# A convolution and an expert layer in one kernel: parts of 28 rows of tokens in place of 14, and more blocks of four units

## The chip, the cores and the metric

The kernel runs on one core of a Trainium2 chip. The time is that of one execution on the device, in microseconds (us); 1278.25 is the median of three runs before the change (1277.03 to 1278.94). A core has five engines that run side by side, each through its own list of instructions in order: PE (matmuls), DVE (vector), ACT (activation), POOL (here: scatters and a few sums) and SP (issues most DMAs). An instruction waits at the head of its engine until the semaphores that it names are reached, and everything behind it waits too.

## What is computed

```python
w = softmax(weight, -1)                       # 8 heads x 7 taps
x = sum over k of w[h, k] * x_pad[b, s + k]   # causal, (8, 3584, 192)
logits = x @ w_gate                           # 8 experts
local_gate = sigmoid(x @ w_local)
for b, s:                                     # e is kept along a sequence
    e = argmax(logits[b, s]) if s == 0 or local_gate[b, s] < 0.5 else prev_e
    out[b, s] = softmax(logits[b, s])[e] * (relu(x[b, s] @ w1[e]) @ w2[e])
    prev_e = e
```

The heads have 24 channels each, w1 is 192 x 1024 and w2 is 1024 x 192 for each expert, all in fp32. Tokens number 28672. A token takes the expert of the token before it unless its own gate opens, so routing is a scan along each sequence of 3584.

## The kernel before

**Parts.** Tokens are worked through in 16 parts of 1792, two to a sequence. Parts 0 and 1 are convolved on PE at the start (`wide`, `wide_route`). The others are convolved by `conv` on DVE: a partition holds 14 tokens in a row with a halo of 6, laid out as six chunks of 32 channels; for each chunk ACT makes the first tap and DVE adds six, each an operation of 128x448 (L441). `route` then takes the logits on PE (`logits`, L632), turns the convolved rows to token order on DVE (L642), scans the experts and works out for each token a slot in a table in DRAM, sorted by expert. `put` scatters one row of 128 tokens into `slots`, on POOL (L846): 14 of them a part.

**Blocks.** The expert layer runs over units of 128 tokens of one expert, in blocks: singles (one unit) first, then pairs, then quads (four units, `seven` and `output_late`), and at the end late pairs and late singles for what is left in each expert. `table` finds after each part which full units there are and which expert each block takes. `ONE`, `TWO` and `MID` say how many blocks of a kind have to be there after part g; `_sure` counts those that exist whatever the routing, `_likely` those that exist if the routing is not far out. A block that was only likely may stay empty; as many spare blocks (`LOSE`, `SPARE`) stand behind an `if` at the end. Each block loads the w1 and w2 of its expert, 1.5 MB.

**Order.** All instructions are recorded in one hand-made order, the order of each engine's list. The loop over blocks calls `hidden` and `output` (or `seven` and `output_late`), and in between `step(time)`: it takes convolution or routing operations from two generators (`conv`, `route`) until their planned times (0.68 for an L441 operation, 0.2 for a small one) fill the given time. So `step`'s numbers say how much of DVE's side work stands in each block. `start_route` waits until the rows tile is free (`rows_free`), `start_conv` until the part before has been turned. `spots` in `output` name the matmuls behind which a `put` follows. `ensure(i)` loads the rows of the blocks after i (`load_rows`); when those of the next one or two blocks still lack scatters, it records the missing `put`s on the spot. `load_rows` waits for all scatters of its part.

**Buffers.** x of a part has two tiles; the rows in token order have three (`row_tile`), z (the convolved part) two, and the quads' rows take over one of them.

Of the kernel before, what the change touches and what calls it, by code (L numbers as in the profile page):

```python
# [8 lines left out]
F32 = mybir.dt.float32  # L9
I32 = mybir.dt.int32  # L10
# [14 lines left out]
NT = 14  # L25
PT = P * NT
NPART = N // PT
PER = S // PT
# [18 lines left out]
EARLY = 2  # L47
SINGLES = 21
# [9 lines left out]
def _likely(tokens, size, left):  # L58
# [7 lines left out]
NARROW = 8  # L66
PAIRED = 46
# [20 lines left out]
LOSE = 4 * LOST + 2 * LOST2  # L88
# [7 lines left out]
TQ = (NT + 3) // 4  # L96
WA = F * KD // 2
# [14 lines left out]
def kernel(  # L112
# [118 lines left out]
    def z_tile():  # L231
        return yt.tile([P, 3 * NH * TB + NB * DR], F32, name="z")
# [181 lines left out]
    def conv(g, x_sb):  # L414
        z = (z_tile() if g % 2 else
             ys[2].tile([P, NB, DG], F32, name="y_sb").rearrange("p b d -> p (b d)"))
        z = z[:, :NT * D].rearrange("p (b s) -> p b s", b=DQ)
# [16 lines left out]
        for b in range(DQ):  # L434
            at["b"] = b
            firsts(0 if 0 < st["block"] < TURNED else 1)
            if b == {3: 3, 4: 3}.get(g, 1) and 2 < g < NPART - 1:
                x_in[g + 1] = load_x(g + 1)
                st["loaded"] = st["block"]
            for k in range(1, KC):  # L440
                nc.vector.scalar_tensor_tensor(z[:, b, :], chans(b, k), c[:, b, k:k + 1],  # L441
                                               z[:, b, :], Alu.mult, Alu.add)
                yield 0.68
# [168 lines left out]

    def gathered(ps):
        xg = xp.tile([P, KT, DG], F32, name="xg")
# [4 lines left out]
    def logits(g, z):  # L619
# [27 lines left out]
        nc.vector.transpose(lq.rearrange("p t e -> p (t e)"), ls.rearrange("p h x -> p (h x)"))
        yield 0.4
        lt = sm.tile([P, NT, E + 1], F32, name="lt")
        aside = g > ASIDE and (st["cgen"] is not None or not late_p)  # L650
        if aside and late_p:
            yield "hop"
        for r in range(4):
# [11 lines left out]
            if aside:  # L665
                yield "hop"
        return y_sb, lt

    def route(g):
        y_sb, lt = yield from logits(g, got.pop(g))  # L670
# [3 lines left out]
        yield 0.3  # L674
        ex = sm.tile([P, NT, E], F32, name="ex")
        nc.vector.tensor_tensor(ex, lg, bcast(mx, E), op=Alu.subtract)
        yield 0.3

        eq = sm.tile([P, NT, E], F32, name="eq")
        nc.vector.scalar_tensor_tensor(eq, ex, 0.0, bcast_mid(ed, NT), Alu.is_equal, Alu.mult)  # L680
        yield 0.3
        key = sm.tile([P, NT], F32, name="key")
        nc.vector.tensor_reduce(key, eq, axis=AX.X, op=Alu.max)
        yield 0.3
# [3 lines left out]
        if g % PER == 0:  # L688
# [971 lines left out]
```

## Time and profile before

| | |
|---|---|
| median of three runs | 1278.25 us |
| the profiled execution | 1279.44 us, its span 1277.7 us |
| granted PE clock | 0.996 |
| DVE convolution operations (L441) | 504 of 0.70 us |
| DMAs of weights | 105 of 1536 KB, 12 of 512 KB |
| scatters into slots | 228 |

The page's first part gives each engine's busy time and share of the span; its second cuts the span into 40 slices (a digit is tenths of busy time). The view by stages lists for each stretch its length, then for each engine the busy time with its number of records, the granted PE clock, the share of the DMA engines and GB/s. In the timeline and in the chain a row has its start, its length, engine, line, what is written `<-` what is read, the number of instructions merged, and in brackets the idle time before it with what ended it. A matmul in fp32 leaves two records. In a group's row the two numbers behind the first bar are busy us in all and the mean of one in ns.

### The profile page before, as it was taken

What the parts mean: (1) busy time and instruction counts of PE and PEld (TensorE: products, weight loads), DVE (VectorE), ACT (ScalarE), POOL (GpSimd) and SP (SyncE); (2) the same over time, 40 slices, a digit from 0 to 9 for tenths busy, and PEclk for the clock granted to TensorE, in tenths of its full rate; (3) what the DMA queues carried; (4) which work ended last, traced back from release to release, by engine and by line L of the source; (5) the groups of instructions that cost most, each with busy time, mean ns of one, the idle gap of its engine ahead of it and who ended that gap; (6) DMA issues with size and microseconds to landing.
All of it is one profiled execution on the core that took longest, in us unless ns stands there. A gap on an engine that the chain in (4) does not pass through costs nothing.

```text
span 1277.7 us, 39046 instructions
## 1 busy us (share of the span) xinstructions
PE 1251.7 (98%) x15186; PEld 1204.5 (94%) x15186; DVE 957.8 (75%) x2507; ACT 535.5 (42%) x1164; POOL 556.9 (44%) x619
## 2 busy tenths in 40 slices
PE   8899999999999999999999999999999999999997
PEld 7889998999999999999999999999999999999996
DVE  6989887999998989999899989985886443431111
ACT  5445542333343442434434544544444453432332
POOL 4544452434344444444446355536456533321211
PEclk9999999999999999999999999999999999999998
DMA  5799988979798898979897564636466464456894
GB/s 202 266 368 417 360 292 284 343 231 308 222 296 263 256 288 239 292 251 270 284 243 232 120 176 125 179 103 195 131 163 178 137 168 126 124 154 199 259 302 155
DMA packets 185810, 293.96 MB, mean 230 GB/s; under 512 B 150416, under 2 KB 160839, under 8 KB 170386
## 3 DMA queue, kind: packets, MB, share of 16 engines
q1 hardware_dynamic: 163296, 246.18, 61.5%
q0 software_dynamic: 22320, 45.22, 10.8%
q8 instruction: 121, 1.98, 0.6%
q14 instruction: 71, 0.58, 0.1%
q10 hardware_dynamic: 2, 0.00, 0.0%
HBM read 245.75 MB, written 46.07 MB: 228 GB/s over the span
## 4 chain that ended last, share of the span: by engine, by line
PE 83%; DVE 9%; DMA 4%; issue 2%; POOL 0%; SPq 0%; ACT 0%; DVEq 0%; POOLq 0%
PE ps L1299 22%; PE yps L1102 19%; PE hps L1078 18%; PE ps L1249 14%; PE ps L1194 4%; PE xps L1249 3%; DVE y_sb L441 2%; DMA wb<-in_w_dram 2%; DVE z L441 1%; DMA hot<-slots 1%; DMA y_sb<-slots 1%; PE xps L632 1%; DVE o_sb L1116 1%; PE hps L252 1%; DMA slots<-y_sb,posi 1%
## 5 line engine op out<-in xcount | busy, mean ns | idle before, releaser
L1130 POOL DMA_INDIRECT out_dram<-o_sb,head x208 | 215.3, 1035 | 455.7 <-DVE o_sb L1314 265.8
L1102 PE MATMUL yps<-wb,hT 64*128 64x192 f32 x3616 | 317.6, 324 | 5.3 <-DVE o_sb L1116 4.8
L1078 PE MATMUL hps<-xT,wb 64*128 64x256 f32 (+1 forms) x3216 | 312.5, 344 | 1.3 <-issue 1.1
L1102 PEld LDWEIGHTS yps<-wb,hT 64*128 64x128 f32 x3616 | 302.0, 187 | 12.1 <-DVE o_sb L1116 9.9
L1299 PE MATMUL ps<-wb,hot 64*128 64x192 f32 x3712 | 310.6, 323 | 0.0
L846 POOL DMA_INDIRECT slots<-y_sb,posi x228 | 232.4, 1019 | 167.6 <-PE yps L1102 70.8
L1299 PEld LDWEIGHTS ps<-wb,hot 64*128 64x128 f32 x3712 | 302.3, 187 | 3.0 <-issue 0.6
L1078 PEld LDWEIGHTS hps<-xT,wb 64*128 64x128 f32 x3216 | 280.9, 187 | 21.3 <-issue 1.6
L1087 ACT ACTIVATE hT<-hps 128x512 f32<-128x512 f32 (+1 forms) x268 | 127.4, 527 | 164.0 <-PE hps L1078 163.9
L441 DVE SCALAR_TENSOR_TENSOR z<-x_sb,c,z 128x448 f32<-128x448 f32 x252 | 175.1, 704 | 12.2 <-ACT z L428 6.1
L441 DVE SCALAR_TENSOR_TENSOR y_sb<-x_sb,c,y_sb 128x448 f32<-128x448 f32 x252 | 174.0, 700 | 10.8 <-ACT y_sb L428 4.9
L1314 DVE SCALAR_TENSOR_TENSOR o_sb<-ps,head,o_sb 128x192 f32<-128x192 f32 x116 | 43.5, 412 | 125.2 <-ACT o_sb L1309 119.9
L1309 ACT ACTIVATE o_sb<-ps,head 128x192 f32<-128x192 f32 x116 | 43.2, 417 | 204.9 <-PE ps L1299 204.9
L1112 ACT ACTIVATE o_sb<-yps,head 128x192 f32<-128x192 f32 x92 | 33.6, 417 | 163.0 <-PE yps L1102 162.9
L1173 DVE STREAM_TRANSPOSE xT<-y_sb 128x768 f32<-128x768 f32 (+1 forms) x65 | 55.2, 877 | 62.1 <-PE ps L1194 28.6
L1249 PE MATMUL ps<-xT,wb 64*128 64x256 f32 x736 | 88.6, 377 | 0.0
L1249 PEld LDWEIGHTS ps<-xT,wb 64*128 64x128 f32 x736 | 77.5, 187 | 1.2 <-issue 0.4
L1194 PE MATMUL ps<-xT,wb 64*128 64x128 f32 (+1 forms) x912 | 67.3, 300 | 0.9 <-DVE xT L1173 0.9
L1194 PEld LDWEIGHTS ps<-xT,wb 64*128 64x128 f32 x912 | 65.2, 188 | 1.8 <-DVE xT L1173 1.8
L1270 DVE TENSOR_TENSOR hot<-xps,hot 128x512 f32<-128x512 f32 x46 | 31.5, 685 | 42.0 <-PE xps L1249 42.0
L1271 ACT ACTIVATE hot<-hot 128x512 f32<-128x512 f32 x46 | 29.0, 630 | 64.3 <-DVE hot L1270 64.3
L1059 DVE STREAM_TRANSPOSE xT<-hot 128x768 f32<-128x768 f32 x46 | 44.6, 971 | 9.7 <-DMA hot<-slots 9.6
(301 smaller groups left out, 1363.5 us busy)
## 6 DMA issues: line engine op xcount, KB each, us to landing
wb<-in_w_dram SPq DMA_DIRECT2D x105, 1536.0 KB
x_sb<-in_x_dram SPq DMA_DIRECT2D x14, 1920.0 KB
hot<-slots SPq DMA_DIRECT2D x184, 96.0 KB
y_sb<-slots SPq DMA_DIRECT2D x92, 192.0 KB
wb<-in_w_dram SPq DMA_DIRECT2D x12, 512.0 KB
slots<-y_sb,posi POOLq DMA_INDIRECT x228
out_dram<-o_sb,head POOLq DMA_INDIRECT x208
x_sb<-in_xb_dram SPq DMA_DIRECT2D x4, 768.0 KB
```

Source lines behind the costliest of these rows:

```text
L441: nc.vector.scalar_tensor_tensor(z[:, b, :], chans(b, k), c[:, b, k:k + 1], z[:, b, :], Alu.mult, Alu.add)
L846: ins = nc.gpsimd.indirect_dma_start(out=slots[:, :], in_=rows, in_offset=None, out_offset=bass.IndirectOffsetOnAxis(ap=to, axis=0)).ins
L1059: nc.vector.transpose(xT.rearrange("p d (j t) -> p j d t", t=Q), xgs[i][0].rearrange("p j (d t) -> p j d t", t=Q))
L1078: ins = nc.tensor.matmul(hps[half][:, j, w], lhsT=wb[rows, w1 + f0:w1 + f0 + P], rhs=xT[rows, d, w], start=(d == 0 and j == 0), stop=(d == ...
L1087: nc.scalar.activation(hT[:, m:m + 2, w], hps[half][:, :, w], Act.Relu)
L1102: ins = nc.tensor.matmul(yps[half][:, k * D:(k + 1) * D], lhsT=hT[rows, m, k * P:(k + 1) * P], rhs=wb[rows, w2 + m * D:w2 + (m + 1) * D], ...
L1130: sent = nc.gpsimd.indirect_dma_start(out=out, in_=o, in_offset=None, out_offset=bass.IndirectOffsetOnAxis(ap=xg.bitcast(I32)[:, k, 1:2], ...
L1173: nc.vector.transpose(xT.rearrange("p d (j t) -> p j d t", t=Q)[:, js], rows[:, js].rearrange("p j (d t) -> p j d t", t=Q))
L1194: nc.tensor.matmul(hps[:, half, j, :], lhsT=wb[rows, f0:f0 + P], rhs=xT[rows, d, :], start=(d == 0 and j == 0), stop=(d == KD - 1), skip_g ...
L1249: ins = nc.tensor.matmul(to[:, half, j, :], lhsT=b[rows, j * P:(j + 1) * P], rhs=a[rows, :], start=(first and j == 0), stop=True, skip_gro ...
L1299: ins = nc.tensor.matmul(yps[:, half, k * D:(k + 1) * D], lhsT=h[two][rows, side, j, k * P:(k + 1) * P], rhs=wb[rows, f * D:(f + 1) * D], ...
L1314: nc.vector.scalar_tensor_tensor(o_sb[:, k, :], yps[:, 1, k * D:(k + 1) * D], xg[:, at + k, 0:1], o_sb[:, k, :], Alu.mult, Alu.add)
```

## The change

Parts 2 to 15 become seven parts of a whole sequence: 28 tokens in a row on each partition (`NT`), still six chunks, with operations of 128x896 (L472 in the new file). Seven tiles' worth of buffers become one tile, `arena`, in which places are given by hand: six chunk places for x, each loaded again for the next part as soon as its convolution is over (`load_chunk`, one DMA a chunk); one z; three halves of a part's rows as a ring (`row_tiles`, `H_AT`), of which a part takes two; a place for the quads' rows and one for temporaries. `so_far` is no longer carried from part to part, as a part is a sequence.

The blocks are 23 singles, 20 pairs, 28 + 8 quads, 4 late pairs and 42 late singles of which 28 are spare; before they were 21, 46, 19 + 4, 5 and 34 of which 20 are spare. Two of the singles and three of the first 12 pairs are now likely and no longer sure. 7, 14 and 23 singles come from the two halves of sequence 0 as before, 12 pairs from sequence 1, 8 from sequence 2, then 7 quads from each of the next four.

The times of `step` change: 2.2 + 2.8 planned us in a single (before 2.1 + 1.2 + 1.3), 3.9 + 1.2 + 3.3 in a pair (before 4.2 + 1.2 + 3.4), 10.7 in a quad as before; a 128x896 operation counts as 1.15. `spots` get more places for scatters, as 28 of them follow each route.

```diff
-NT = 14
-PT = P * NT
-NPART = N // PT
+PT = P * 14
+NT = 28
+EARLY = S // PT
+NPART = EARLY + (N - S) // (P * NT)
...
-PAIRED = 46
+PAIRED = 20
...
+    def load_chunk(g, b):
+        if g < NPART:
+            nc.sync.dma_start(out=spot(X_AT + b * XN, XN),
+                              in_=x[g - EARLY, :, b * XN:(b + 1) * XN])
...
-        return ys[(0, 1, 3)[g % 3] if g < NARROW else g % 2].tile([P, NB, DG], F32, name="y_sb")
+        return spot(g * YN, YN).rearrange("p (b d) -> p b d", d=DG)
+
+    def row_tiles(g):
+
+        return [spot(H_AT[(2 * (g - EARLY) + k + 2) % 3], HN).rearrange("p (b d) -> p b d", d=DG)
+                for k in range(2)]
...
-        return not any(p[0] <= (g - 3 if g < NARROW else g - 2) for p in to_put)
+        return (not any(p[0] <= g - 2 for p in to_put)
+                and (g == EARLY or sum(p[0] == g - 1 for p in to_put) <= HT))
...
-            if b == {3: 3, 4: 3}.get(g, 1) and 2 < g < NPART - 1:
-                x_in[g + 1] = load_x(g + 1)
-                st["loaded"] = st["block"]
+            load_chunk(*((g, b + 4) if b < 2 else (g + 1, b - 2)))
             for k in range(1, KC):
                 nc.vector.scalar_tensor_tensor(z[:, b, :], chans(b, k), c[:, b, k:k + 1],
                                                z[:, b, :], Alu.mult, Alu.add)
-                yield 0.68
+                yield 1.15
...
-        if to_put and to_put[0][0] == 3:
+        if n == 1 and len(to_put) > 3 * (TURNED - 1 - st["block"]):
+            spots[2, 0, 7] = 0
+        if to_put and (to_put[0][0] == EARLY or n > 1 and len(to_put) > HT):
...
-            if j >= FIRST and j > i + 2:
+            if j >= FIRST and j > i + 2 or j > FIRST > i:
                 return
...
-            step((2.4, 0)[i] if i < 2 else 2.1 if n == 1 else 4.2 if i < FIRST - 1 else 3.0)
+            step((2.4, 0)[i] if i < 2 else 2.2 if n == 1 else 3.9 if i < FIRST - 1 else 3.0)
...
-                step(1.3 if n == 1 and i != 1 else 3.4)
+                step(3.4 if i == 1 else 2.8 if n == 1 else 3.3)
```

How the instructions stand, at two places. First POOL, at the end of the singles. `slots<-` are scatters of rows (`put`), `out_dram<-o_sb,xg` the outputs of singles, `out_dram<-o_sb,head` those of pairs; the brackets hold what an instruction waits for. Before, from the output of the last single to the first of the first pair:

```order
L1130 DMA out_dram<-o_sb,xg 28672x192 [waits DMAHW2_49,DMASW0_49,DVE_49]
L846 DMA slots<-y_sb,posi 230528x195 [waits DMASW1_49,PE_49]
L846 DMA slots<-y_sb,posi 230528x195 [waits DMASW2_49,PE_49]
L846 DMA slots<-y_sb,posi 230528x195 [waits DMASW3_49,PE_49]
L846 DMA slots<-y_sb,posi 230528x195 [waits DMASW4_49,PE_49]
L846 DMA slots<-y_sb,posi 230528x195 [waits DMASW5_49,PE_49]
L1130 DMA out_dram<-o_sb,head 28672x192 [waits DMAHW1_49,DMASW6_49,DVE_49]
```

With the change, the last rows of the singles and the first of the pairs:

```order
L876 DMA slots<-arena,posi 230528x195 [waits DMASW5_49,PE_49]
L876 DMA slots<-arena,posi 230528x195 [waits DMASW6_49,PE_49]
L876 DMA slots<-arena,posi 230528x195 [waits DMASW7_49,PE_49]
L1157 DMA out_dram<-o_sb,xg 28672x192 [waits DMAHW7_49,DMASW0_49,DVE_49]
L876 DMA slots<-arena,posi 230528x195 [waits DMASW1_49]
L1157 DMA out_dram<-o_sb,xg 28672x192 [waits DMAHW1_49,DMASW2_49,DVE_49]
L1157 DMA out_dram<-o_sb,head 28672x192 [waits DMAHW3_49,DMASW3_49,DVE_49]
```

Before, the scatters between the last single and the first pair belong to part 3, while the first pair takes rows of part 2, scattered blocks earlier. Now the one scatter between the outputs of singles 21 and 22 is the last of part 2 (all of sequence 1), recorded by `ensure` and so with no matmul to stand behind; the first pair's rows are loaded behind it.

Second DVE, in a quad beside convolution. `hot<-` are the sums of the first layer, `xT<-` the transposes of the next block's rows, `xg`, `xT` and `hT` from `xT` the next block's combined rows, `o_sb` the outputs. Before, from one block's transposes on:

```order
L1173 STREAM_TRANSPOSE xT<-y_sb 128x8x3x32 x2
L441 SCALAR_TENSOR_TENSOR y_sb<-x_sb,c,y_sb 128x448 x10
L1314 SCALAR_TENSOR_TENSOR o_sb<-ps,head,o_sb 128x192 x2
L1224 TENSOR_TENSOR xg<-xT 128x256
L1225 TENSOR_TENSOR xT<-xT 128x256
L1226 TENSOR_TENSOR xg<-xT 128x256
L1228 TENSOR_TENSOR hT<-xT,xg 128x256
L1229 TENSOR_TENSOR hT<-xT 128x256
L441 SCALAR_TENSOR_TENSOR y_sb<-x_sb,c,y_sb 128x448 x3
L1314 SCALAR_TENSOR_TENSOR o_sb<-ps,head,o_sb 128x192 x2
L441 SCALAR_TENSOR_TENSOR y_sb<-x_sb,c,y_sb 128x448 x3
L1270 TENSOR_TENSOR hot<-xps,hot 128x512
```

With the change:

```order
L1198 STREAM_TRANSPOSE xT<-arena 128x8x3x32 x2
L472 SCALAR_TENSOR_TENSOR arena<-arena,c 128x896 x6
L1339 SCALAR_TENSOR_TENSOR o_sb<-ps,head,o_sb 128x192 x2
L1249 TENSOR_TENSOR xg<-xT 128x256
L1250 TENSOR_TENSOR xT<-xT 128x256
L1251 TENSOR_TENSOR xg<-xT 128x256
L1253 TENSOR_TENSOR hT<-xT,xg 128x256
L1254 TENSOR_TENSOR hT<-xT 128x256
L472 SCALAR_TENSOR_TENSOR arena<-arena,c 128x896
L1339 SCALAR_TENSOR_TENSOR o_sb<-ps,head,o_sb 128x192 x2
L472 SCALAR_TENSOR_TENSOR arena<-arena,c 128x896 x2
L1295 TENSOR_TENSOR hot<-xps,hot 128x512
```

Where 16 operations of 448 stood between two blocks' transposes, 9 of 896 stand now, at the same three places.

More of the change, by code (lines that the diff above doesn't have):

```diff
@@ L24 @@
 UT = 128
-NT = 14
-PT = P * NT
-NPART = N // PT
-PER = S // PT
+PT = P * 14
+NT = 28
+HT = NT // 2
+EARLY = S // PT
+NPART = EARLY + (N - S) // (P * NT)
+TOK = [PT * (g + 1) if g < EARLY else S + P * NT * (g + 1 - EARLY) for g in range(NPART)]
 HALO = KC - 1
@@ L46 @@
 DUMMY = E * CAPU
-EARLY = 2
-SINGLES = 21
 SPARE = 2
@@ L96 @@
 TQ = (NT + 3) // 4
+YN = NB * DG
+HN = HT * DG
+RN = QT // Q * D2
+R_AT = 2 * HN
+H_AT = (0, HN, R_AT + RN)
+XN = NX * Q
+X_AT = H_AT[2] + HN
+Z_AT = X_AT + DQ * XN
+ZN = NT * Q
+TMP_AT = Z_AT + DQ * ZN
+ZW = 3 * NH * TB + NB * DR
+TMP = (("ls", 2 * TQ * Q), ("lq", 2 * TQ * Q), ("lt", NT * (E + 1)), ("ex", NT * E), ("eq", NT * E),
+       ("oh", NT * E), ("at", NT * E))
+ARENA = TMP_AT + sum(n for _, n in TMP)
 WA = F * KD // 2
@@ L664, in logits @@
                     yield 0.12
-            if aside:
+            if aside and r % 2:
                 yield "hop"
-        return y_sb, lt
+        return y_sbs, lt
     def route(g):
-        y_sb, lt = yield from logits(g, got.pop(g))
+        y_sbs, lt = yield from logits(g, got.pop(g))
         lg = lt[:, :, :E]
@@ L813, in route @@
         for t in range(NT):
-            to_put.append((g, y_sb[:, t, :], posi[:, t:t + 1]))
+            to_put.append((g, y_sbs[t // HT][:, t % HT, :], posi[:, t:t + 1]))
         yield 0.2
@@ L1061, in turn_pair @@
         return xT
-    def few():
-        return to_put and to_put[0][0] == 2 and st["block"] % 2 == 0
     def hidden(n, wb, xT, w1):
@@ L1082, in hidden @@
                     held.pop(0)(ins)
-                if n == 1 and (two, d) == (0, 0) and st["block"] and not (st["hot"] or few()):
+                if n == 1 and (two, d) == (0, 0) and st["block"] and not st["hot"]:
                     put(ins)
@@ L1147, in ring @@
             return flat[:, at:at + n * UT // Q * D2].rearrange("p (j d) -> p j d", d=D2)
[L1148 to L1151 removed]
+        flat = room["rows"] if (i - FIRST) % 2 else spot(R_AT, RN)
+        return flat[:, :n * UT // Q * D2].rearrange("p (j d) -> p j d", d=D2)
     def make_room():
@@ L1157, in make_room @@
             room[f"h{k}"] = flat[:, k * 4 * HU * P:(k + 1) * 4 * HU * P]
-        small = [xp.tile([P, KT, DG], F32, name="xg").rearrange("p k d -> p (k d)")[:, :HU * P]
-                 for _ in range(5)]
+        small = [xp.tile([P, HU * P], F32, name="xg") for _ in range(5)]
         room["wt"], room["xc"] = small[:3], small[3:]
@@ L1164, in more_room @@
         room["xc"] += [flat[:, k * HU * P:(k + 1) * HU * P] for k in range(2)]
+        room["rows"] = flat[:, 2 * HU * P:]
     def turn_late(n, rows):
@@ L1324 @@
     late_p = []
-    LATE = 3
     SIDE = (2.4, 4.5, 2.0, 1.8)
     st = {"block": 0, "conv": 1, "cgen": None, "route": 1, "rgen": None, "routed": 1,
-          "due": False, "hot": False, "since": 0, "bank": None, "over": 0, "turned": 1, "loaded": 0}
+          "due": False, "hot": False, "since": 0, "bank": None, "over": 0, "turned": 1}
     def start_conv():
         g = st["conv"] + 1
-        if (st["cgen"] is None and g < NPART and g <= st["turned"] + 2
-                and (late_p or g < 4 or st["block"] > st["loaded"] + 2)
-                and (g != 3 or g in x_in and st["block"] > LATE + 2)):
+        if st["cgen"] is None and g < NPART and g <= st["turned"] + 1:
             st["conv"] = g
-            st["cgen"] = conv(g, x_in.pop(g))
+            st["cgen"] = conv(g)
             next(st["cgen"])
@@ L1376, in step @@
             elif c == "pe":
-                st["due"], st["since"], go = True, st["block"] - early, False
+                st["due"], go = True, False
+                st["since"] = st["block"] - (early or time > 1.5)
             elif c == "hop":
@@ L1383, in step @@
                 time -= c + 0.05 if go and late_p else c
-        st["over"] = min(time, 1.5) if late_p else 0
+        st["over"] = min(time, 1.5) if late_p else min(time, 0)
     ya, yb = row_tile(0), row_tile(1)
@@ L1541, in between @@
                 held.pop(0)(ins)
-            if n == KQ and part and two and k == 0 and len(to_put) > NT // 2:
+            if n == KQ and len(to_put) > ((HT, HT // 2)[part] if k == 0 else HT) and two:
                 put(ins)
```

150 lines of the change are left out of this document (74 added, 76 removed).

## The prediction

> **What bounds the kernel now.** I read the page's busy shares and slices first, then the chain that ended last.
>
> ```profile
> PE 1251.7 (98%) x15186; PEld 1204.5 (94%) x15186; DVE 957.8 (75%) x2507; ACT 535.5 (42%) x1164; POOL 556.9 (44%) x619
> PE   8899999999999999999999999999999999999997
> DVE  6989887999998989999899989985886443431111
> PE 83%; DVE 9%; DMA 4%; issue 2%; POOL 0%; SPq 0%; ACT 0%; DVEq 0%; POOLq 0%
> ```
>
> PE is busy in every slice, and 83% of the chain is PE. So the time is, nearly, the sum of PE's matmuls; DVE is second and nearly full in the first 29 slices (up to about 930 us), where it convolves and routes. The change is therefore priced twice: what it does to PE's sum, and what it does to the places where PE waits.
>
> For PE's sum I took the price of each kind of block from the chain in order of time and from PE's timeline, from stretches without a wait.
>
> ```profile
> 145.00 2.85 PE L1078 MATMUL hps<-xT,wb 64*128 64x128 f32 x48
> 150.44 2.85 PE L1078 MATMUL hps<-xT,wb 64*128 64x128 f32 x48
> 341.20 5.18 PE hps L1078 x48
> 351.58 5.18 PE hps L1078 x48
> 1111.25 10.40 PE ps L1299 x128
> 1131.17 10.40 PE ps L1299 x128
> 132.39 1.68 PE L632 MATMUL hps<-z,wg 64*32 64x128 f32 x96
> 134.00 2.95 PE L1078 MATMUL hps<-xT,wb 64*128 64x128 f32 x48
> ```
>
> From start to start: a single takes 150.44 - 145.00 = 5.44 us, a pair 351.58 - 341.20 = 10.38, a quad 1131.17 - 1111.25 = 19.92, and the logits of one part 134.00 - 132.39 = 1.6. A quad is 0.84 us cheaper than two pairs (its first layer has 44 matmuls in place of 48).
>
> The waits come from the view by stages: singles, pairs (two rows), quads (two rows), late pairs, late singles.
>
> ```profile
> core 0: us, PE busy (x) PEld busy (x) DVE busy (x) ACT busy (x) POOL busy (x), PEclk, DMA share, GB/s
> 46.20:172.70 126.50, 122.18 (x1951) 118.17 (x1952) 113.77 (x350) 66.84 (x205) 59.85 (x59) 1.00 0.90 341
> 172.70:303.00 130.30, 126.06 (x1482) 121.12 (x1480) 114.57 (x314) 42.26 (x89) 56.52 (x56) 1.00 0.88 298
> 303.00:673.10 370.10, 370.10 (x4542) 349.16 (x4543) 343.69 (x950) 151.20 (x380) 168.33 (x166) 1.00 0.85 265
> 673.15:902.50 229.35, 226.65 (x2669) 218.57 (x2668) 197.50 (x424) 109.53 (x184) 118.30 (x124) 1.00 0.57 159
> 902.50:1141.40 238.90, 238.90 (x2595) 235.41 (x2593) 133.34 (x314) 103.12 (x145) 107.34 (x117) 1.00 0.54 149
> 1193.30:1277.70 84.40, 74.91 (x1123) 73.72 (x1120) 14.04 (x29) 25.06 (x72) 15.55 (x16) 0.96 0.77 247
> ```
>
> Singles: 126.5 - 21 x 5.44 - 2 logits x 1.6 = 9 us lost. Pairs: 500.4 - 46 x 10.38 - 9 x 1.6 = 8.5 lost. Quads: 468.3 - 23 x 19.92 - 3 x 1.6 = 5.3 lost, all before 902.5. These 23 us are what the change can add to or take from beside PE's sum.
>
> **The change, part by part.**
>
> *1. Other blocks.* Both programs put 229 units of 128 tokens through PE outside the spare blocks: 21 singles, 46 pairs, 23 quads, 5 late pairs, 14 late singles before; 23, 20, 36, 4, 14 now. So 27 pairs go (-280.3), 13 quads (+259.0) and 2 singles (+10.9) come: **-10.4 us**, all on PE, the bound.
>
> *2. Half as many logits.* 7 parts in place of 14, each with as many matmuls of 224 columns in place of 128. The first layer's 48 matmul records take 5.18 us at 256 columns and 2.85, with a tail, at 128, so time goes by columns: 1.6 x 1.75 = 2.8 us a part. 7 x 2.8 - 14 x 1.6 = **-2.8**. If columns cost nothing it would be 7 x 1.6, so -11.2; dearer than by columns nothing here suggests.
>
> *3. DVE's convolution.* No row shows a 128x896 operation, so it is bounded.
>
> ```profile
> L441 DVE SCALAR_TENSOR_TENSOR z<-x_sb,c,z 128x448 f32<-128x448 f32 x252 | 175.1, 704 | 12.2 <-ACT z L428 6.1
> L1270 DVE TENSOR_TENSOR hot<-xps,hot 128x512 f32<-128x512 f32 x46 | 31.5, 685 | 42.0 <-PE xps L1249 42.0
> L1273 DVE TENSOR_TENSOR hot<-ps,hot 128x1024 f32<-128x1024 f32 x23 | 28.1, 1222 | 2.9 <-PE ps L1249 2.9
> L1116 DVE SCALAR_TENSOR_TENSOR o_sb<-yps,xg,o_sb 128x192 f32<-128x192 f32 x21 | 8.6, 410 | 2.2 <-ACT o_sb L1112 2.2
> ```
>
> Twice 704 = 1.41 us if all of it goes by size; and 0.94 if there is no fixed part at all (896 at the 1.05 ns an element of the other two rows, (1222 - 685) / 512). I take 704 + 448 x 1.05 = 1.17, since that slope is of the same engine and type. A part of 28 rows then costs 36 x 1.17 = 42 us where two parts of 14 cost 72 x 0.70 = 50.
>
> [...]
>
> *Singles.* By the order DVE has 30 convolution operations in the seven last full singles, 4.3 each: 4.3 x 1.17 + 0.4 for the output (fourth row) = 5.4 us, level with PE's 5.44. Before it was 8 of 0.70 + 0.4 = 6.0 in such blocks, longer than PE's. I take 5 us lost in place of 9, most of it in the first four blocks, which stay: **-4** (bounds -9 and +12, the latter with 1.41).
>
> *Pairs.* 7.1 operations, one transpose (0.98) and two outputs (0.74): 10.0 us, just inside 10.38. Before, 14 x 0.70 + 1.7 = 11.5. I take 2 lost in place of 8.5: **-6.5** (bounds -8.5 and +4).
>
> *Quads.* This goes the other way, as more quads run with convolution beside them.
>
> ```profile
> 705.20:726.50 21.30, 20.40 (x218) 19.55 (x217) 20.39 (x31) 13.64 (x32) 9.73 (x12) 1.00 0.59 152
> 746.50:766.40 19.90, 19.90 (x220) 19.67 (x218) 17.29 (x58) 8.56 (x13) 9.39 (x10) 1.00 0.53 147
> 707.00 7.50 DVE L441 SCALAR_TENSOR_TENSOR y_sb<-x_sb,c,y_sb 128x448 f32<-128x448 f32 x10
> 785.84 1.14 PE L1249 MATMUL ps<-xT,xg 64*128 64x256 f32 x8 [1.27 <-DVE hot L1273]
> ```
>
> The quad from 705.2 has 16 convolution operations (10 in the third row) and lasts 21.3 us; that from 746.5 has routing instead and lasts 19.9. A quad full of convolution is DVE's: in the last row PE waits 1.27 us for DVE's sum. DVE's other work in it is 21.3 - 16 x 0.70 = 10.1. In the order of the change, seven quads have 8 to 10 operations: four with 9, 10.1 + 10.5 = 20.6 (+0.7 each); two with 10, 21.8 (+1.9 each); one with 8 and ten small ones of routing, 21.5 (+1.6): 8.2, and with about 0.6 at each of three logits 10. So 10 lost in place of 5.3: **+4.7** (bounds -5 and +20).
>
> *4. The hand-over from singles to pairs: a wait that is new.* The first pair now needs all of sequence 1. Its 28th scatter stands on POOL behind the output of single 21, which waits for DVE's `o_sb` of that block. SP's load of the pair's rows waits for this scatter, DVE's transpose for the load, and PE for the transpose. On DVE the output of single 22 and part 3's transposes are queued behind it, on SP the next weights; they are three blocks early. The same chain stands once in the trace; the last two rows show a shorter landing.
>
> ```profile
> 187.55 0.99 POOL L1130 DMA_INDIRECT out_dram<-o_sb,head  x1 [0.30 <-issue]
> 194.98 0.96 POOL L846 DMA_INDIRECT slots<-y_sb,posi  x1 [0.30 <-issue]
> 201.60 2.23 SPq L1007 DMA_DIRECT2D hot<-slots  x4
> 206.08 0.98 DVE L1059 STREAM_TRANSPOSE xT<-hot 128x768 f32<-128x768 f32 x1 [5.04 <-DMA hot<-slots]
> 207.16 5.45 PE L1078 MATMUL hps<-xT,wb 64*128 64x256 f32 x48 [1.07 <-issue]
> 383.43 0.96 POOL L846 DMA_INDIRECT slots<-y_sb,posi  x1 [2.58 <-DMA hot<-slots]
> 385.55 2.23 SPq L1007 DMA_DIRECT2D hot<-slots  x4
> ```
>
> From the scatter's issue to the load's it took 6.6 us and 2.1 us; from load to transpose 4.5, and 1.1 more to PE. Ahead of it stand the output's scatter (first row) and two gaps, 1.6. The whole is 13.8 us by the longer landing, 9.3 by the shorter. Beside it PE has about 7.4 us (the rest of single 22 and part 3's logits). So 2 to 6.4 us are lost; I take **+4**, and keep 0 and 8 as ends.
>
> [...]
>
> *5. Nothing.* Routing has the same small operations a part, for half the parts, and none of them stood on PE's chain by a row above. ACT's first taps are as many bytes in half the instructions, on an engine that is 42% busy; x comes in six chunks of a part, each loaded four chunks (24 operations, 28 us of DVE) ahead, and DMA is the less loaded the fewer pairs there are (0.88 and 0.85 in pairs, 0.57 and 0.54 in quads). If that cover were gone, DVE would wait for a chunk's landing, 5 us as above, once per part at most. The late singles keep their 84.4 us.
>
> *The sum*: -10.4 - 2.8 - 4 - 6.5 + 4.7 + 4 = -15.0. The span of 1277.7 becomes 1262.7, the profiled execution's 1279.4 becomes 1264.4. That execution lies 1.2 us over the median of 1278.25, so the median becomes **1263**.
>
> **Rivals.**
>
> *All is hidden.* The scatter lands in 2.1 us, as at 383.43, and DVE's operation costs 1.05, midway between 0.94 and 1.17. Then the hand-over costs 0 and the quads lose 4 (10.1 + 9 x 1.05 is under 19.92): 1263 - 4 - 6 = 1253. For it speaks that most landings of the pair stage are short; against it the row at 194.98, in the same crowded stretch as the hand-over. 15%. [...]
>
> *The waits fall at their dear end.* Hand-over 8, quads 15, singles as before: 1263 + 4 + 5 + 4 = 1276, no difference or just faster. For it speaks that DVE is within 0.3 us of PE in every stage. 12%.
>
> *DVE becomes the bound* (slower than before). If the 896 operation costs 1.41 us, singles take 4.3 x 1.41 + 0.4 = 6.5 us and 16 of them lose 1.0 each, eight pairs lose 1.3 each, seven quads 2.2 each: +42, so 1305. Each 0.01 us over 1.17 costs about 1.3 us, over 1.22 about 1.9, so the gain of 15 is gone at 1.27. Against it stand the rows of 685 and 1222 ns, which double the size for 1.78 times the time. 6%.
>
> *The change doesn't do what it says.* The first 12 pairs are now taken for likely, not sure. If one stayed empty, its 10.4 us are spent for nothing and two spare singles follow at the end, one after another, at 84.4 / 14 = 6 us or more each: +22, 1285. Counting the reference's routing of these inputs gives just 12 pairs there, the tightest expert with 7 tokens over, so no. 2%.
>
> **How the numbers follow.** The forecast, 1257 to 1270, has 65%. The range of 1252 to 1275 takes in the first rival and most of the second. A measurement of this kernel tells 0.2% (2.6 us) from no change: faster 0.88 (forecast, first rival, most of the second), the same 0.05, slower 0.07 (the last two rivals and an edge of the second).
>
> **What would show it.** The new operation's mean at 1.17 us; 7 logits of 2.8 us; full quads at 19.92 us in the last dozen and near 20.7 where nine convolutions stand beside; a PE wait of about 4 us for `xT` at some 180 us; pairs at 10.38. It would be wrong if the operation is over 1.25 us, if PE waits for rows at the start of other stages, or if the spare blocks run.

## The result, and the profile after

| | before | after |
|---|---|---|
| median | 1277.9 us (4 runs) | 1300.92 us (1298.86 to 1301.87, 4 runs) |
| ratio to before | 1 | 1.0178 (95%: 1.016 to 1.0195) |
| span of the profiled execution | 1277.7 us | 1300.2 us |
| mean granted PE clock | 0.996 | 0.988 |

The change makes the kernel 1.8% slower, 38 us over the forecast of 1263. First the page of the changed kernel: busy time, PE's and DVE's slices, the granted clock, and the group of the new convolution operation.

```profile
PE 1244.4 (96%) x14466; PEld 1201.5 (92%) x14466; DVE 884.1 (68%) x1738; ACT 554.6 (43%) x1065; POOL 629.4 (48%) x671
...
PE   9889997999999899999999999999999999999997
...
DVE  6985975895995799878996999968744344441111
...
PEclk9999998999999899999999999999999999999999
...
L472 DVE SCALAR_TENSOR_TENSOR arena<-arena,c 128x896 f32<-128x896 f32 x252 | 296.9, 1187 | 25.6 <-ACT arena L461 20.5
```

PE's busy time fell by 7.3 us (1251.7 before) and DVE's by 73.7 (957.8 before), the operation costs 1187 ns where 1170 was forecast, and yet the span grew by 22.5. So neither PE's nor DVE's work became more. POOL's did, by 72.5 us (556.9 before): the sums of 36 quads in place of 23 are 41 us of it, and its 457 scatters, the same number in both kernels, took 31 us longer in all. Those into `slots`, before and after:

```profile
L846 POOL DMA_INDIRECT slots<-y_sb,posi x228 | 232.4, 1019 | 167.6 <-PE yps L1102 70.8
L876 POOL DMA_INDIRECT slots<-arena,posi x228 | 252.3, 1107 | 107.6 <-issue 37.6
```

PE has new gaps, and two of its slices (the seventh and the fourteenth) were granted less than 0.9 of the clock. The view by stages of the changed kernel shows where: singles, the hand-over to pairs, pairs with the hand-over to quads, quads beside convolution and routing, and quads behind them.

```profile
core 0: us, PE busy (x) PEld busy (x) DVE busy (x) ACT busy (x) POOL busy (x), PEclk, DMA share, GB/s
46.47:193.30 146.83, 133.95 (x2025) 130.46 (x2025) 116.68 (x226) 75.85 (x231) 77.25 (x69) 0.99 0.93 356
193.30:203.18 9.88, 2.50 (x97) 1.85 (x97) 1.03 (x2) 1.02 (x3) 2.07 (x3) 0.85 0.37 91
203.18:427.67 224.49, 217.28 (x2432) 203.32 (x2432) 170.62 (x322) 84.50 (x189) 106.75 (x98) 0.98 0.80 256
427.67:895.78 468.11, 454.31 (x5041) 438.06 (x5043) 405.50 (x760) 213.28 (x319) 265.77 (x260) 0.99 0.59 168
895.78:1174.69 278.91, 278.91 (x3028) 275.72 (x3027) 136.98 (x279) 120.07 (x168) 133.22 (x145) 1.00 0.54 152
```

A stage's length less its blocks at the undisturbed 5.44, 10.38 and 19.92 us, and less 2.44 us for each part's logits in it, is what it lost:

| stage | blocks and logits | lost before | forecast | lost after |
|---|---|---|---|---|
| singles | 23 and 1 | 9 | 5 | 146.83 - 125.12 - 2.44 = 19.3 |
| hand-over to pairs | 0 and 1 | 0 | 4 | 9.88 - 2.44 = 7.4 |
| pairs | 20 and 2 | 8.5 | 2 | 224.49 - 207.60 - 4.88 = 12.0 |
| quads with side work | 22 and 3 | 5.3 | 10 | 468.11 - 438.24 - 7.32 = 22.6 |
| quads without | 14 | 0 | 0 | 278.91 - 278.88 = 0 |

That is 61.3 us where 21 were forecast, so 40.3 more: 14.3 in the singles, 12.6 in the quads, 10.0 in the pairs and 3.4 at the hand-over. The logits give 2.5 back (2.44 us each where 2.8 was forecast), which makes 37.8; the span missed its 1262.7 by 37.5. The late blocks behind the quads took 125.5 us, 10.8 less than before for one late pair less, so no spare block ran. What PE waited for, in the view of its waits, with total, number and longest:

```profile
PE yps L1129 <- ACT hT L1112: 7.4, 6, 2.6
PE hps L1103 <- DVE xT L1088: 7.4, 1, 7.4
PE xps L422 <- DMA xg<-slots: 7.1, 2, 4.4
PE ps L1274 <- DVE hot L1298: 5.7, 6, 1.4
PE ps L1274 <- DVE xT L1198: 4.9, 1, 4.9
PE ps L1274 <- DVE xT L1250: 4.1, 5, 1.8
PE ps L1274 <- POOL wb L1233: 2.1, 1, 2.1
```

These come to 38.7 us; the rest of the 61 is small gaps and matmuls that ran slower behind a wait. The timeline of the changed kernel at six such places, in order of time:

```profile
91.11 0.47 PE L422 MATMUL xps<-ident,xg 64*128 64x64 f32 x4 [4.39 <-DMA xg<-slots]
91.35 4.37 PE L1129 MATMUL yps<-wb,hT 64*128 64x192 f32 x32
...
117.64 2.03 ACT L695 COPY arena<-arena 32x63 f32<-32x63 f32 x8 [2.50 <-DVE arena L681]
119.69 1.21 ACT L1112 ACTIVATE hT<-hps 128x256 f32<-128x256 f32 x4
120.13 2.87 PE L1129 MATMUL yps<-wb,hT 64*128 64x192 f32 x32 [2.65 <-ACT hT L1112]
...
177.92 0.42 ACT L1139 ACTIVATE o_sb<-yps,xg 128x192 f32<-128x192 f32 x1 [4.59 <-DMA out_dram<-o_sb,xg]
...
189.71 0.41 DVE L1143 SCALAR_TENSOR_TENSOR o_sb<-yps,xg,o_sb 128x192 f32<-128x192 f32 x1
...
193.72 0.99 POOL L1157 DMA_INDIRECT out_dram<-o_sb,xg  x1 [0.30 <-issue]
195.01 0.96 POOL L876 DMA_INDIRECT slots<-arena,posi  x1 [0.30 <-issue]
...
198.19 1.88 SPq L1036 DMA_DIRECT2D hot<-slots  x4
...
202.15 0.98 DVE L1088 STREAM_TRANSPOSE xT<-hot 128x768 f32<-128x768 f32 x1 [10.96 <-DMA hot<-slots]
...
203.18 7.37 PE L1103 MATMUL hps<-xT,wb 64*128 64x256 f32 x48 [7.38 <-DVE xT L1088]
...
417.00 0.96 POOL L876 DMA_INDIRECT slots<-arena,posi  x1 [0.30 <-issue]
...
426.64 1.84 DVE L1198 STREAM_TRANSPOSE xT<-arena 128x768 f32<-128x768 f32 x2 [8.48 <-DMA arena<-slots]
427.67 2.67 PE L1274 MATMUL ps<-xT,wb 64*128 64x256 f32 x10 [4.86 <-DVE xT L1198]
...
565.74 1.84 DVE L1198 STREAM_TRANSPOSE xT<-hT 128x768 f32<-128x768 f32 x2 [2.18 <-DMA hT<-slots]
567.50 7.07 DVE L472 SCALAR_TENSOR_TENSOR arena<-arena,c 128x896 f32<-128x896 f32 x6
574.48 0.74 DVE L1339 SCALAR_TENSOR_TENSOR o_sb<-ps,head,o_sb 128x192 f32<-128x192 f32 x2
```

1. At 91 us the rows of single 7 come late (4.39 us of wait), and the 32 matmuls behind the wait take 4.37 us, not 2.85.
2. At 117 us ACT makes eight small copies of part 2's logits (2.03 us), and `hT` of the running single stands behind them: PE waits 2.65 us. The same again costs 2.19 us in the second pair, at 223.
3. At 177.9 us ACT's output has waited 4.59 us for the scatter of an older output, since its buffer is still being read; POOL is behind.
4. Single 21's output is there at 190.1 us, but POOL reaches its scatter at 193.72 and the last scatter of part 2 at 195.01. From this last one to PE it takes 8.2 us more. The wait is 7.38 us, and the first pair's 48 matmuls take 7.37 us, where those of later pairs take 5.35.
5. The first quad waits in the same way for rows that need the scatter of 417.00. POOL is not full there (gaps of 0.6 to 2.9 us between its scatters from 397 to 415 us); it is 10.7 us from this scatter to PE.
6. In the first whole quad behind a part's logits DVE stands 2.18 us for rows, then runs six convolution operations, and the block's output (574.48) stands behind them.

### The profile page after: what moved, and what is told of

Read it like the earlier page. It is cut to its first block, busy times and chain, and to the rows that moved or that the text cites. A ratio compares the mean times of both kernels' runs of the same rounds, so it can differ in the third digit from the quotient of the medians.

```text
span 1300.2 us, 36582 instructions
## 1 busy us (share of the span) xinstructions
PE 1244.4 (96%) x14466; PEld 1201.5 (92%) x14466; DVE 884.1 (68%) x1738; ACT 554.6 (43%) x1065; POOL 629.4 (48%) x671
## 4 chain that ended last, share of the span: by engine, by line
PE 72%; DMA 7%; DVE 6%; issue 2%; ACT 1%; POOL 1%; SPq 1%; DVEq 0%; POOLq 0%; ACTq 0%
PE ps L1324 29%; PE ps L1274 17%; PE yps L1129 9%; PE hps L1103 8%; PE ps L1219 4%; PE xps L1274 4%; DVE arena L472 2%; DMA slots<-arena,posi 2%; DMA arena<-slots 1%; DMA hT<-slots 1%; DVE o_sb L1339 1%; DMA wb<-in_w_dram 1%; SPq L1036 1%; DVE xT L1198 1%; DMA out_dram<-o_sb,xg 1%
## 5 line engine op out<-in xcount | busy, mean ns | idle before, releaser
L1324 PE MATMUL ps<-wb,hot 64*128 64x192 f32 x5312 | 443.9, 323 | 0.0
L1324 PEld LDWEIGHTS ps<-wb,hot 64*128 64x128 f32 x5312 | 433.6, 187 | 4.6 <-issue 1.1
L472 DVE SCALAR_TENSOR_TENSOR arena<-arena,c 128x896 f32<-128x896 f32 x252 | 296.9, 1187 | 25.6 <-ACT arena L461 20.5
L876 POOL DMA_INDIRECT slots<-arena,posi x228 | 252.3, 1107 | 107.6 <-issue 37.6
L1129 PE MATMUL yps<-wb,hT 64*128 64x192 f32 x2016 | 180.3, 329 | 7.6 <-ACT hT L1112 7.4
L1103 PE MATMUL hps<-xT,wb 64*128 64x128 f32 (+1 forms) x2064 | 178.2, 323 | 7.9 <-DVE xT L1088 7.4
L1129 PEld LDWEIGHTS yps<-wb,hT 64*128 64x128 f32 x2016 | 170.8, 190 | 11.2 <-ACT hT L1112 9.1
L1103 PEld LDWEIGHTS hps<-xT,wb 64*128 64x128 f32 x2064 | 161.3, 189 | 20.2 <-DVE xT L1088 7.8
L1112 ACT ACTIVATE hT<-hps 128x256 f32<-128x256 f32 (+1 forms) x172 | 72.8, 481 | 91.4 <-PE hps L1103 91.2
L1274 PE MATMUL ps<-xg 64*128 64x256 f32 x576 | 76.1, 376 | 0.1
L1198 DVE STREAM_TRANSPOSE xT<-hT 128x768 f32<-128x768 f32 (+1 forms) x45 | 39.1, 900 | 37.3 <-PE ps L1219 13.9
```

Source lines behind the costliest of these rows:

```text
L876: ins = nc.gpsimd.indirect_dma_start(out=slots[:, :], in_=rows, in_offset=None, out_offset=bass.IndirectOffsetOnAxis(ap=to, axis=0)).ins
L1103: ins = nc.tensor.matmul(hps[half][:, j, w], lhsT=wb[rows, w1 + f0:w1 + f0 + P], rhs=xT[rows, d, w], start=(d == 0 and j == 0), stop=(d == ...
L1112: nc.scalar.activation(hT[:, m:m + 2, w], hps[half][:, :, w], Act.Relu)
L1129: ins = nc.tensor.matmul(yps[half][:, k * D:(k + 1) * D], lhsT=hT[rows, m, k * P:(k + 1) * P], rhs=wb[rows, w2 + m * D:w2 + (m + 1) * D], ...
L1198: nc.vector.transpose(xT.rearrange("p d (j t) -> p j d t", t=Q)[:, js], rows[:, js].rearrange("p j (d t) -> p j d t", t=Q))
L1274: ins = nc.tensor.matmul(to[:, half, j, :], lhsT=b[rows, j * P:(j + 1) * P], rhs=a[rows, :], start=(first and j == 0), stop=True, skip_gro ...
```

## The experiments

The theory: PE's sum came out as forecast, and the loss is waits at places where something now arrives too late (rows behind POOL's queue and DMA's backlog, `hT` behind ACT's copies, quads' sums behind DVE's convolution), some of them made longer by a slower PE behind the wait. The rivals: the new mix of blocks is what costs; the clock falls by itself. Ratios are to the kernel before, run beside each kernel on the same chip; the first two groups ran on chips where that takes 1278 to 1279 us. The changed kernel's 1.0178 is the measure.

**The mix: 46 pairs with parts of 28.**

```diff
-PAIRED = 20
+PAIRED = 46
```

> The changed kernel with 46 pairs as before (23 singles, 46 pairs, 23 quads), so parts of 28 rows without the new mix. PE's sum is 10.9 us above that of the changed kernel. Theory (waits at the hand-over to pairs, behind ACT's queue and for late loads in the singles; DVE full in the quads): the waits before the second pair stay, about 20 us over the forecast, the quads lose 8 to 12 us less, as fewer of them have convolution beside them: 1298 to 1304 us. Rival (the new mix is what costs, quads above all): near the kernel before, 1275 to 1282.

1286.42 us, 1.0053 (1.0036 to 1.007). Both missed: the mix carries more than the theory said, though not all. The waits ahead of the second pair stay, as the theory had it (8.3 us for rows in the singles, 7.9 at the first pair, 7.1 behind ACT's `hT`). Its two stages of pairs and quads, in the view by stages:

```profile
203.88:701.92 498.04, 495.53 (x5633) 464.97 (x5635) 409.58 (x826) 184.41 (x400) 257.84 (x234) 0.99 0.85 262
701.92:1161.83 459.91, 458.43 (x4970) 452.01 (x4970) 223.14 (x438) 197.23 (x276) 197.54 (x217) 1.00 0.56 148
```

The pairs (46, with five logits) lose 498.04 - 477.48 - 12.2 = 8.4 us and hold all the convolution that is left; the 23 quads lose 459.91 - 458.16 = 1.8, and there is no hand-over wait in front of them. So the mix with 20 pairs saves 10.9 us of PE's sum, and for that the quads lose 20.8 us more (2.5 of it in a slow first quad) and the wait for the first quad's rows costs 4.9.

**DVE in the quads: half of the taps left out from the sixth part on.**

```diff
-                nc.vector.scalar_tensor_tensor(z[:, b, :], chans(b, k), c[:, b, k:k + 1],
-                                               z[:, b, :], Alu.mult, Alu.add)
+                if g < 5 or k % 2: nc.vector.scalar_tensor_tensor(
+                    z[:, b, :], chans(b, k), c[:, b, k:k + 1], z[:, b, :], Alu.mult, Alu.add)
```

> The changed kernel without half of DVE's convolution operations from the sixth part on (taps 2, 4 and 6 are left out there, so later tokens are convolved with four taps; 18 operations a part, 21 us, less on DVE, everything else in the same order). Theory: the quads beside convolution lose 20 us because DVE has 10 us of other work and up to ten operations in them: with 3 to 5 operations they fall to 19.92 us, and the time to 1300.9 - 14 to 18, so 1283 to 1287. Rival (quads lose to late rows, POOL's or ACT's queue): 1294 or more.

The total is 1484.37 us, and the forecasts for it are void: other values route other tokens, so blocks at the end that else stand idle behind their `if` are run. What can be read is the stretch of quads, which run in the same order whatever the routing. From the second quad to the block behind the last logits, in the view by stages, here without half of the taps:

```profile
450.26:857.24 406.98, 406.87 (x4612) 396.90 (x4610) 302.03 (x571) 196.32 (x296) 238.64 (x243) 1.00 0.62 175
```

and in the changed kernel:

```profile
450.06:870.93 420.87, 409.80 (x4611) 395.89 (x4610) 362.25 (x622) 196.56 (x296) 248.76 (x243) 1.00 0.59 170
```

13.9 us less, with 60 us less on DVE, and nearly no gap left on PE (406.87 of 406.98). In this stretch of 20 quads and three logits, which lost 15.2 us, DVE's convolution is what the quads lose to, as the theory said. The quad behind it, the second one behind the last logits, has no convolution beside it and lasts 24.64 us in this run too (24.85 in the changed kernel). In its rows DVE makes the last part's copies (3.13 us) ahead of the outputs, and PE then waits 2.1 us for POOL's sums; that these are its cause is read from the rows and not tried.

**ACT's copies: on DVE in singles and pairs.**

```diff
-        aside = g < LAST
+        aside = g < LAST and bool(late_p)
```

> The changed kernel, but the 16 small copies of a part's logits are DVE's in the singles and pairs, as before, and ACT's in the quads alone. Theory: ACT's queue (8 copies 2.0 us, beside a first tap of 1.04) is what PE waited for at 120.1 (2.65 us) and 223.1 (2.19 us), and each wait brings some 2 us of slower matmuls behind it: both vanish, DVE pays 3 us a part in two places: 1300.9 - 4 to 8, so 1293 to 1297. Rival (ACT waits for something else there, DVE has no room in the singles): 1300 or more.

It is the change that put these copies on ACT in the singles. Before, `aside` was `g > ASIDE and ...` with `ASIDE = 5`, so that the copies of parts 2 to 5 were DVE's, and ACT made those of later parts four at a time; with the change it is `g < LAST`, eight at a time. Neither the list of changes nor the prediction speaks of this line. Two rows of the kernel before, a part beside the singles and the first one on ACT:

```profile
138.36 2.68 DVE L663 COPY lt<-lq 32x36 f32<-32x36 f32 x14
313.11 0.90 ACT L661 COPY lt<-lq 32x36 f32<-32x36 f32 x4 [2.78 <-DVE lq L647]
```

1293.30 us, 1.0118 (1.0101 to 1.0135): some 7.7 us better, by the theory. PE's waits behind ACT's `hT` fall from 7.4 to 1.8 us in all. 1.8 us are given back at the first pair, which now waits 9.18 us, as part 3's logits no longer stand beside that wait.

**The late rows of single 7: part 3's chunks loaded later.**

```diff
-            load_chunk(*((g, b + 4) if b < 2 else (g + 1, b - 2)))
+            load_chunk(*((g, b + 4) if b < 2 else (g + 1 if g > EARLY else NPART, b - 2)))
...
-        weights(i + AHEAD)
+        weights(i + AHEAD); load_chunk(EARLY + 1, i - 8) if 8 <= i < 12 else None
```

> The changed kernel, but the first four chunks of the third part are loaded beside singles 8 to 11 in place of 3 to 7. Theory: the wait of 4.39 us for the rows of single 7 is DMA's backlog, which these chunks made; it vanishes, and the 1.9 us of slower matmuls behind it: 1300.9 - 4 to 6, so 1295 to 1297. Rival (the backlog is the weights' and the second part's): the wait stays within 1 us, 1300 to 1301.

1296.48 us, 1.0143 (1.0126 to 1.016): 4.5 us better. The wait at single 7 is 1.29 us, and no slow matmuls follow. SP issues the loads of these rows at the same time in both runs (85.14 and 85.38 us), and PE has them 6.0 us later in the changed kernel and 2.0 us later here. So the new chunks were the backlog that held them.

**A slower PE behind a wait: idle products in the two gaps.**

```diff
-        st["block"] = i
+        st["block"] = i; awake({TURNED: 26, FIRST: 16}[i]) if i in (TURNED, FIRST) else None
```

> The changed kernel with 26 idle products of 128 columns on PE ahead of the first pair and 16 ahead of the first quad (about 0.25 us each), no other change. They fill the two waits for rows (7.38 and 4.86 us) without ending them sooner. Theory: PE's matmuls run slower for some 5 us behind a wait because PE stood still, so the first pair lasts 10.4 in place of 12.4 and the first quad 20 in place of 22.4: 1300.9 - 4.5, so 1296 to 1297. Rival (the clock falls there by itself, or for the load on the chip): no gain, 1300 to 1302.

1298.53 us, 1.0159 (1.0142 to 1.0176): not the 1296 to 1297 of the theory, and not to be told from the changed kernel by the time alone. What the products do is plain in the rows; the timeline of PE at the first pair:

```profile
195.27 6.07 PE L209 MATMUL hps<-ones 128*128 128x128 f32 x52
202.28 5.45 PE L1103 MATMUL hps<-xT,wb 64*128 64x256 f32 x48 [0.94 <-DVE xT L1088]
```

The pair's 48 matmuls take 5.45 us where they took 7.37, although their rows came only 0.9 us sooner. In the stretches from 200 to 205 us the granted clock is

```profile
200.00:205.00 5.00, 4.06 (x39) 3.60 (x39) 3.75 (x4) 0.00 (x0) 0.99 (x1) 1.00 0.65 133
```

here, and in the changed kernel

```profile
200.00:205.00 5.00, 1.82 (x8) 1.52 (x10) 2.85 (x4) 0.00 (x0) 0.99 (x1) 0.53 0.65 134
```

so 1.00 against 0.53: the clock did not fall by itself there, PE's standing still brought it down. It did not follow each wait. The second pair's 64 matmuls behind 2.19 us take 7.15 us in the changed kernel (granted clock 0.74 from 225 to 230 us) and 5.47 here (1.00 from 222 to 227). In the changed kernel's singles waits of 2.70 us (at 58) and 2.65 us (at 120) were followed by stretches at 1.00, and the 3.44 us in the run with 24 singles, below, by 48 matmuls in 5.45 us. What makes the difference between these waits no run shows.

**POOL's queue: seven output scatters left out.**

```diff
-            if k == 0 and not st["hot"]:
+            if n == 1 and 14 <= st["block"] <= 20: pass
+            elif k == 0 and not st["hot"]:
```

> The changed kernel without the seven output scatters of singles 14 to 20 (their tokens are not written out; POOL has 7 x 1.27 = 9 us less to issue). Theory: POOL is full from 143.5 us to 196 and so issues the last scatter of the second part 5 us after the output of single 21 is there; with room it follows that output at once, and the wait of 7.38 us at the first pair falls to 3 or 4: 1295 to 1298. Rival (DVE's output of single 21 alone sets the last scatter): the wait stays within 1 us, 1300 to 1301.

1295.61 us, 1.0136 (1.0115 to 1.0156): 5.4 us better, as the theory has it for the time. Its timeline:

```profile
187.28 0.96 POOL L876 DMA_INDIRECT slots<-arena,posi  x1 [0.30 <-issue]
...
191.23 2.54 SPq L1036 DMA_DIRECT2D hot<-slots  x4
...
196.09 0.98 DVE L1088 STREAM_TRANSPOSE xT<-hot 128x768 f32<-128x768 f32 x1 [9.97 <-DMA hot<-slots]
...
197.13 8.33 PE L1103 MATMUL hps<-xT,wb 64*128 64x256 f32 x48 [5.43 <-DVE xT L1088]
```

The last scatter comes 7.7 us sooner than in the changed kernel, and ACT's waits for output buffers in the last singles are gone. But the wait at the first pair is still 5.43 us, not 3 to 4: from the scatter to PE it now takes 9.9 us, and PE too arrives 4.1 us sooner, mostly since the last singles no longer wait behind ACT. So most of the gain lies in the singles, and not at the wait from which the theory took it. POOL sets the scatter; the landing sets the rest.

**The hand-over: 24 singles, and four scatters in each.**

```diff
-LEFT1 = E * (UT // 2 + UT // 16)
+LEFT1 = E * (UT // 2)
...
-        if n == 1 and len(to_put) > 3 * (TURNED - 1 - st["block"]):
+        if n == 1 and len(to_put) > 0:
```

> The changed kernel with 24 singles (then 20 pairs, 35 quads, 5 late pairs, 15 late singles: PE's sum +1.2 us) and four scatters of the second part in each single until all are out. Theory: the last scatter comes about a block before it is needed, the wait at the first pair and the 2 us of slower matmuls behind it vanish: 1300.9 - 7.4 - 2 + 1.2 = 1292 to 1294. Rival (POOL cannot issue five in a single, its backlog holds back the outputs of the singles instead): 1299 to 1304.

1286.62 us, 1.0066 (1.0049 to 1.0083): 14.3 us better, twice what was expected. The wait for rows at the first pair is gone (3.44 us for weights stand in its place, without slow matmuls behind), and so is that in the second pair, as part 3's logits have moved a block ahead. At the first quad a wait of 3.75 us behind POOL's sums takes the place of that for rows, and the quad behind the last logits lasts 20.4 us, not 24.9.

The wait for the rows of single 7 is gone as well, without the later chunks of the run above. The edit hastens every scatter in the singles, also those of the first sequence that single 7 needs, so that SP issues its load 3.4 us sooner. The changed kernel's row stands first, then this run's:

```profile
85.14 1.25 SPq L1028 DMA_DIRECT2D xg<-slots  x2
81.71 0.33 SPq L1028 DMA_DIRECT2D xg<-slots  x1
```

Only the wait at the first pair was foreseen, so this run says more on how such places hang together than on the one that it was made for.

**All of it, with 46 pairs.** The edits of the runs with 46 pairs, ACT's copies, later chunks and 24 singles, together.

> 46 pairs, the small copies of the logits on DVE in singles and pairs, the third part's chunks beside singles 8 to 11, and 24 singles with four scatters each, together. From 1286.4 with 46 pairs: ACT's two waits -4 to -7, the late rows -4, the hand-over -7 to -8. Theory: 1268 to 1273, below the kernel before. Rival (the gains share one cause, or one takes the cover of another): 1277 to 1283.

1271.58 us, 0.9947 (0.9931 to 0.9964): the theory's range, and 0.5% faster than the kernel before beside it. Of the changed kernel's waits behind rows in singles and at both hand-overs only 2.9 us are left; three behind ACT's `hT` remain, again where its output buffer waits for POOL.

**Four output buffers, 20 pairs with all remedies, 40 pairs.** These fell on three other chips, on which the kernel before itself takes 1300 to 1309 us, so only runs beside one another are compared. The changed kernel was run on one of them as well; with four buffers the edit is `bufs=2` to `bufs=4` in the pool `op`.

> The changed kernel itself once more, as the measure for the three runs beside it. If the runs of this call are like those of the first chips: 1.018 of the kernel before. If they are like those of the last call, where the kernel before took 1306 us and PE stood 20 times and more for its next instruction, it shows what the change costs there: 1.02 to 1.03.

> The changed kernel with four output buffers, against the changed kernel on the same chip. Theory (POOL's queue sets the hand-over to pairs): the three waits behind ACT in the last singles vanish, the wait at the first pair grows by as much, and the time is within 2 us. Rival (DVE's output of single 21 sets it): 2.5 to 4 us faster.

> The changed kernel's mix of 20 pairs with the four remedies for singles and hand-over. Theory: 16 to 20 us faster than the changed kernel, still 3 to 7 us slower than the kernel before, since the quads beside convolution are left as they are. Rival (without the waits ahead the mix is worth its 10.9 us): 35 us faster than the changed kernel, 10 faster than before.

> 46 pairs, the remedies, and four output buffers. Theory: the three waits behind ACT (7.0 us with two buffers) go and nothing takes their place: 0.989 to 0.991 of the kernel before, 4 to 6 us below the same with two buffers (0.9947). Rival (POOL's queue is what counts, the wait moves to the first pair): 0.993 to 0.996.

Beside one another on that chip: the changed kernel 1.0238 (1.0205 to 1.0272), four buffers 1.0205 (1.0182 to 1.0227), 20 pairs with the remedies 1.0166 (1.015 to 1.0182), 46 pairs with the remedies and four buffers 1.0115 (1.0089 to 1.0141). On the two other chips of this kind four buffers gave 1.0244 and 1.0228, 46 pairs with all 1.0086 and 1.0102, 20 pairs 1.0228. What had been forecast for these from the times of the first chips (1264 to 1267 us for 46 pairs, 1281 to 1285 for 20) missed. On one of the two 40 pairs were run as well:

> The same with 40 pairs: PE's sum is 2.5 us lower, but the last 30 us or so of convolution fall beside two quads in place of three pairs. Theory (a quad beside convolution loses 1 to 2 us): 0.5 us below the run with 46 pairs to 2 above it. Rival (the loss in the quads begins only with a whole part beside them): 2 to 3 us below it.

40 pairs 1.0088 (1.0055 to 1.0121), the same as 46 beside it (1.0086); the intervals are too wide to tell theory from rival. The waits of PE in the run with 1.0115 show what is different there:

```profile
PE hps L1103 <- issue: 7.7, 21, 0.9
PE ps L1274 <- issue: 5.9, 5, 2.9
PE yps L1129 <- issue: 4.0, 10, 0.9
```

PE stands for its next instruction, for which the profile names no other engine; it does so for 13 to 26 us in all the runs on these chips, and in the changed kernel's first profile not at all. What holds: 20 pairs with the remedies are faster than the changed kernel, by some 9 us where 16 to 20 were expected, and stay slower than before; 46 with the remedies are better than that, and no wait behind ACT's `hT` is over 1.0 us in that run. Four buffers alone gain nothing that can be told, but this says nothing on POOL: on the chip where both were run PE does not wait for rows at the first pair, neither in the changed kernel (first row) nor with four buffers (second row).

```profile
212.84 5.45 PE L1103 MATMUL hps<-xT,wb 64*128 64x256 f32 x48
209.43 5.45 PE L1103 MATMUL hps<-xT,wb 64*128 64x256 f32 x48
```

What does not hold: none of these runs is faster than the kernel before, where 0.989 to 0.991 was expected. Whether the four buffers or these chips take the gain away is open: the run with two buffers was not made there, nor that with four on a chip of the first kind.

## Why the prediction was wrong

- **PE's sum (steps 1 and 2): right.** Blocks took 5.44, 10.38 and 19.92 us in stretches without a wait, the logits 2.44 where 2.8 was forecast. 7 x 2.44 - 14 x 1.6 is -5.3 in place of -2.8.
- **The operation (step 3): right**, 1187 ns for 1170. The 448 elements more cost (1187 - 704) / 448 = 1.08 ns each, where 1.05 was taken from two other rows.
- **Singles (-4): wrong.** They lose 19.3 us, not 5. The step set DVE's work against PE's and stopped there. That part came true: PE's waits behind DVE's `o_sb`, 4.8 us before, are gone. The waits that came are for rows behind DMA and POOL and for ACT.
- **Pairs (-6.5): half wrong.** They lose 12.0 us, not 2. The eighteen behind the second take 10.4 to 10.8 us, nearly as argued. But the first has slow matmuls, the second waits for ACT's copies and the last is followed by a second hand-over, which the prediction looked for at the singles' end only.
- **Quads (+4.7): right in kind, mis-sized.** Of the eight during which DVE ran nine or ten convolution operations, two lost nothing, two 0.9 and 1.1 us and four 1.6 to 1.8; the working had 0.7 and 1.9. So the number of operations alone does not set the loss. 22.6 us were lost in all and not 10, because the second quad behind each part's logits loses 2.4 to 4.9 where 0.6 was put for each logits, and because the first four lose 4.4, of which 2.5 are slow matmuls behind the wait for rows. The run with half of the taps ties 13.9 us of the stage to DVE.
- **The hand-over (+4): the chain was right, its start was not.** From the output's scatter (193.72) to PE it took 9.5 us, at the short end of the 9.3 to 13.8. But this scatter came 3.6 us after DVE's output (190.1), which the chain has at nothing: POOL has 37 scatters in a row there, from 143.5 to 195.0 us, so 1.43 us apart, and is late itself. Beside it PE had 5.7 us of work and not 7.4, so it waited 7.4 us; without POOL's 3.6 it would have been an estimated 3.8. That the 13.1 us in all lie inside the stated bounds is luck.
- **"Nothing" (step 5): this is the step that failed**, together with the terms for singles and pairs, which count DVE alone. It put the queues of ACT and DMA at nothing. Its "same small operations" does not hold: the copies of the early parts went from DVE to ACT. ACT "42% busy" was taken for cover, yet it works in order, and 2 us of copies in front of `hT` were a wait of 2.65 and one of 2.19 us; moving them is worth 7.7 us. "Four chunks ahead" was taken for cover too, and it is those early loads that made single 7's rows late (4.5 us). That POOL's queue is full stands nowhere in the prediction, and more room on POOL was worth 5.4 us.
- **Not priced at all:** that a wait can make PE's next matmuls slower, by 1.5 to 2.5 us each at 91, 203, 223 and 427 us.

Of the rivals, DVE as the bound was the one on the right side, and its 1305 is near the 1301 by luck: the price of the operation on which it rests, 1.41 us, did not come. The dear end, 1276, had the hand-over right (8 us), two thirds of what the quads lose (15), half of what the singles lose (9) and a sixth of what the pairs lose (2).

## What to carry to other kernels

Before a stage is made tighter, list for each engine what stands in its queue ahead of the instruction that the bound engine will wait for: here an engine that was 42% busy still made PE wait (2.65 us behind ACT's copies at 120), as its work is done in order. Where a part doubles, look at each place at which a first block needs all of it, and count the scatters that one queue must issue until then. Moving work to the cheapest block pays only as long as the side engines fit beside it: here the quads saved 0.42 us a pair and cost more than that (20.8 us against 10.9) where DVE had convolution beside them.

## What was not expected of the hardware

Behind four of PE's waits in the changed kernel the granted clock fell, in stretches of 5 us: to 0.74 behind 2.19 us, 0.66 behind 4.39, 0.50 behind 4.86, and behind 7.38 to 0.53 in one stretch and 0.79 in the next. Behind 2.65 and 2.70 us it stayed at 1.00. POOL's scatters, mostly 0.96 us, took up to 1.9 us in places while DVE ran 128x896 operations; that the two belong together was seen side by side only and not tried. And of the five chips of the experiments three ran the kernel before 1.7 to 2.4% slower than the other two, and PE stood for its next instruction in every kernel profiled there; the kernel before was not profiled on them, so that the one makes the other is not shown.
